# Threshold attention and a bilinear FFN on one core: turned weights moved per head, the last block's sums in column halves, VectorE and ScalarE ordered by a list scheduler

## The chip, the core and the metric

The kernel runs on one core of one Trainium2 chip. Its time is the device time of one execution in microseconds (us); lower is better. The engines are named as in the profile: PE is TensorE, PEld its weight load, DVE is VectorE, ACT is ScalarE, POOL is GpSimd, and SP is SyncE, which here does nothing but issue DMAs. Line numbers such as L411 are those of the kernel before.

## The reference

Two layers run one after the other. The first is attention with a threshold: only scores within `tau` of their row's maximum keep a weight. The second is a feed-forward layer that multiplies two projections.

```python
# q, k, v: (8 batches, 8 heads, 576 rows, 64); tau = 0.02
scores = (1 / np.sqrt(64)) * np.matmul(q, k.transpose(0, 1, 3, 2))
thresh = np.max(scores, axis=-1, keepdims=True) - tau
scores = np.where(scores >= thresh, scores, -1000000000.0)
attn = np.exp(scores - np.max(scores, axis=-1, keepdims=True))
attn = attn / (np.sum(attn, axis=-1, keepdims=True) + 1e-09)
out = np.matmul(attn, v)
x = out.transpose(0, 2, 1, 3).reshape(4608, 512)
# w_a, w_b: (512, 1536); w_out: (1536, 512)
return ((x @ w_a) * (x @ w_b)) @ w_out
```

## The kernel before

**Attention.** Heads are taken in pairs, so 32 pairs (8 batches of 4). A unit is a pair and a block of 128 query rows; the rows that are left over, 64 of each head, are put together from two pairs into a unit of their own ("tail", `u == NT`). There are 144 units. The main loop at the end of the kernel runs over slots `g`, one unit in each. A unit goes through these steps:

- `scores` (L404): PE multiplies q by k for both heads into two PSUM tiles `sc`. DVE takes the row maximum (`mx`, L411) and the threshold (`thr`, L412).
- `weigh`: ACT makes a bias (L431) and the exponential (L432); DVE sets to zero what lies under the threshold and sums the rows (L435). That is the last reading of `sc`.
- `reciprocal` and `normalise`: DVE (L446, L448), then ACT scales the weights `tw` by the reciprocal (L454).
- One slot later, `turn_blocks`: DVE transposes the weights within 32x32 blocks (L498), and DMAs write them to a tile `swap` in DRAM. The first eight units are turned on PE instead (`turn_pe`).
- Two slots later, `turn_back`: DMAs read `swap` into `wT`, where the turned weights have the keys on the partitions.
- Three slots later, `weighted` (L542): PE multiplies v by `wT` into a tile `pv`, and `settle` copies it to `xT`, one half by ACT (L549) and the other by DVE (L550).

**Feed-forward layer.** When the heads of 256 rows of a batch are there, they make a block of the layer (`ffn`). There are 18 of them. PE's work on them is laid between the steps of the units in portions (`advance`). Most blocks use a scheme with seven products in place of eight for a part of the projections (`sevens_of`, L720, the rest in L824) and for the output product (L885); sums and differences of operands stand in for the eighth, most of them made by POOL (L682, L853), and on DVE once the loop over the slots is over (`state["over"]`). Output rows leave through `rows_out`, which lists them, and `store`, which sends what is listed.

**The weights at the start.** They arrive in 36 pieces as 64-bit floats and are converted while the first units run: ACT (L298, L299), POOL (L305), DVE (L311, L319), POOL (L324).

**PSUM.** One pool of four buffers, called `banks`, serves all of PE's tiles (`tp`, `sc`, `pv`, `pab`, `po`).

**What sets the order.** `keep_order` ties every instruction to the one before it on its engine, in the order in which the program text emits them; so each engine works through its list in order. From slot 37 on, DMAs are not issued where they are posted: `post` puts them in a list, and `pump` issues from it as PE's columns pass, each tied to the matmul that was emitted last. `flush` issues what a step needs. All these DMAs go out on SP's queue; after the last slot SP and ACT take turns.

Of the kernel before, what the change touches and what calls it, by code (L numbers as in the profile page):

```python
# [37 lines left out]
BY_HEAD = 16  # L38


def keep_order(tc):

    last = {}
    for ins in tc.nc.cur_bb.bb.instructions:
        before = last.get(ins.engine)
        if before is not None:
            tc.add_manual_dep(
                ins, before,
                mybir.DependencyInfo(mybir.DependencyClass.NoSync, mybir.DependencyReason.DATA),
                reason="order")  # L50
        last[ins.engine] = ins.name
# [3 lines left out]
def kernel(  # L55
# [61 lines left out]

    def pool(name, bufs, **kw):
        return ctx.enter_context(tc.tile_pool(name=name, bufs=bufs, **kw))
# [32 lines left out]
    def pump(count=1, paced=True):  # L152

        for _ in range(min(count, len(bulk))):
            behind = next(x.name for x in reversed(nc.cur_bb.bb.instructions) if x.engine == mybir.EngineType.PE)
            for n, move in enumerate(bulk.pop(0)[2]):
                moved = nc.sync.dma_start(*move)
                if n == 0 and paced:
                    tc.add_manual_dep(
                        moved.ins, behind,  # L160
                        mybir.DependencyInfo(mybir.DependencyClass.Sync, mybir.DependencyReason.DATA),
                        reason="pace")
# [38 lines left out]
    def load_v(i, again=False):  # L201
        b, hp = pairs[i]
        if not again:
            loaded[i]["v"] = loads.tile([P, NSLOT, D], FP32, tag="vm", bufs=HP, name="vm")
        for j in range(2):
            rows, half = v[b, 2 * hp + j], loaded[i]["v"][j * D:(j + 1) * D]
            if i >= HP or again:
                if i < HP:
                    rows = rows.rearrange("(c s p) d -> p c s d", c=2, p=Q)
                else:  # L210
                    rows = rows.rearrange("(p c s) d -> p c s d", c=2, p=Q)
                post(("v", i), *((half[c * Q:(c + 1) * Q], rows[:, c]) for c in range(2)))
            else:
                nc.sync.dma_start(half, rows.rearrange("(s p) d -> p s d", p=D))
# [39 lines left out]
    def load_weights(limit, engine=nc.sync, most=NPIECES):  # L254
# [4 lines left out]
        while most and (len(raws) - len(taken) < limit or extra) and state["loaded"] < state["due"]:  # L259
# [7 lines left out]
            for r, part in enumerate(src):  # L267
# [4 lines left out]
                if behind and r == 0:  # L272
                    tc.add_manual_dep(
                        moved.ins, behind,
                        mybir.DependencyInfo(mybir.DependencyClass.Sync, mybir.DependencyReason.DATA),
                        reason="pace")
# [216 lines left out]
    def turn_blocks(i, u):  # L493
# [5 lines left out]
        swap = scratch.tile([G, P, NSLOT * Q], FP32, tag="swap" if u < NT else "swapt", name="swap")  # L499
        swaps[i, u] = swap  # L500
        for g in range(G):
            if u < NT:
                moves = [(swap[g].rearrange("(r p) e -> p r e", p=Q),
                          t[g * Q:(g + 1) * Q].rearrange("p (r s) e -> p r (s e)", r=G))]
            else:
                moves = []
                for m in range(2):
                    j = g // 2 ^ m
                    moves.append((swap[2 * m + g % 2, j * D:(j + 1) * D].rearrange("(r p) e -> p r e", p=Q),
                                  t[g * Q:(g + 1) * Q, m * NB:(m + 1) * NB].rearrange("p (r s) e -> p r (s e)", r=2)))  # L510
            post(("tw", i, u), *moves)

    def turn_back(i, u):

        key = "wT", i, min(u // 2, 1) if i >= HP else u // 2
        if u < NT or i < HP:
            flush(("tw", i, u))
            swap = swaps.pop((i, u)).rearrange("g p e -> p g e")
            turned[i, u] = turned_tile()
            for y in range(0, G, 2):  # L520
                post(key, (turned[i, u][:, y:y + 2].rearrange("p g s e -> p g (s e)"), swap[:, y:y + 2]))
# [277 lines left out]
    def ffn(xT, what):  # L799
# [51 lines left out]
        if state["sums"]:  # L851
# [4 lines left out]
            t1, t2, t4 = (sums_of[:, :, m] for m in range(3))  # L856

# [15 lines left out]
            for both in ((4, 1) if state["all"] else (1, 4), (2, 5), (7, 6), (3,)):  # L873
                po = banks(len(both) * CH, "po").rearrange("p r (m w) -> p r m w", w=CH)
                left = whole = len(both) * NF // 2 * CH
                for m in both:
                    y = sorted(both, reverse=7 in both).index(m)
                    k, u, other = seven[m]
                    for f in range(NF // 2):
                        ht = hs[f // 2 * 2 + k][:, f % 2]  # L880
                        for r in range(2):
                            rows = slice(r * D, (r + 1) * D)
                            for c in range(2):
                                t0 = u * P + c * D
                                nc.tensor.matmul(po[c * D:(c + 1) * D, r, y], ht[rows, t0:t0 + D],  # L885
                                                 other[rows, f], start=(f == 0), stop=(f == NF // 2 - 1))
                        left -= CH
# [4 lines left out]
                        if m == 2 and f == NF // 2 - 1:  # L892
                            h_sums((1, 0), (1, 0), (0, 0), ALU.subtract)
                            state["layer"] = False
                            exchange_blocks()
                        if left:
                            yield CH, left, whole
# [5 lines left out]
                elif 2 in both:  # L903
                    k25 = t
                    pool(k25[:, 0], k25[:, 0], k14[:, 0], op=ALU.add)
                elif 7 in both:
# [7 lines left out]
                else:  # L914
                    if state["over"]:
                        for r, t in enumerate((k76, k25)):
                            nc.vector.tensor_tensor(k25[:, 1], t[:, 1], po[:, r, 0], op=ALU.add)
# [4 lines left out]
                    written(0, k25)  # L922
# [23 lines left out]
    def rows_out(kind, b, h, u, t):  # L946

        if kind != "tail":
            r0 = b * S + h * HALF + u * P
            pending.append((out[r0:r0 + P, :], t))  # L950
        else:
            for e in range(2):
                r0 = (b + 2 * u + e) * S + MAIN
                pending.append((out[r0:r0 + TAIL, :], t[e * TAIL:(e + 1) * TAIL]))
# [102 lines left out]
    n = 0  # L1057
# [135 lines left out]
    keep_order(tc)  # L1193
# [32 lines left out]
```

## Time and profile before

| | |
|---|---|
| Median of 3 runs | 1419.77 us (1418.38 to 1431.88) |
| Span of the profiled execution | 1417.0 us |
| Distance of the median from that span | 2.8 us |
| PE busy | 1370.2 us (97%), 33836 instructions |
| PE weight load busy | 1229.6 us (87%) |
| DVE busy | 1013.7 us (72%), 2200 instructions |
| ACT busy | 679.9 us (48%) |
| POOL busy | 495.7 us (35%) |
| DMA moved | 223.20 MB in 327000 packets, 158 GB/s on average |
| Time of the packets on SP's queue, share of 16 DMA engines' span | 59.2% |
| Mean granted PE clock | 0.994 |

The profiled execution has no time of its own beside its span; the runs' times are 1.4 us and more above the span. Busy time is the time in which at least one instruction of the engine was under way. PE's instructions are two for each matmul of 32-bit numbers. An engine that is idle loses nothing unless the end of the kernel waits for it, so one looks for the engine on which the chain of waits runs, and then for the places where that engine stands still.

### The profile page before, as it was taken

What the parts mean: (1) busy time and instruction counts of PE and PEld (TensorE: products, weight loads), DVE (VectorE), ACT (ScalarE), POOL (GpSimd) and SP (SyncE); (2) the same over time, 40 slices, a digit from 0 to 9 for tenths busy, and PEclk for the clock granted to TensorE, in tenths of its full rate; (3) what the DMA queues carried; (4) which work ended last, traced back from release to release, by engine and by line L of the source; (5) the groups of instructions that cost most, each with busy time, mean ns of one, the idle gap of its engine ahead of it and who ended that gap; (6) DMA issues with size and microseconds to landing.
All of it is one profiled execution on the core that took longest, in us unless ns stands there. A gap on an engine that the chain in (4) does not pass through costs nothing.

```text
span 1417.0 us, 76257 instructions
## 1 busy us (share of the span) xinstructions
PE 1370.2 (97%) x33836; PEld 1229.6 (87%) x33836; DVE 1013.7 (72%) x2200; ACT 679.9 (48%) x1245; POOL 495.7 (35%) x678
## 2 busy tenths in 40 slices
PE   6788999999999999999999999999999999999998
PEld 5677579989878887979998999999888899799997
DVE  6898986778777877776767777677777776744424
ACT  5786554545445454545444545454545455431110
POOL 2674541606060606042333324150606060608100
PEclk9999999999999999999999999999999999999999
DMA  9967776667756775666555675567655775550000
GB/s 212 235 193 219 182 214 163 178 153 183 198 135 173 198 188 155 178 156 184 142 134 149 168 193 158 144 160 199 168 144 152 191 201 154 135 152 18 4 19 18
DMA packets 327000, 223.20 MB, mean 158 GB/s; under 512 B 171536, under 2 KB 310800, under 8 KB 326672
## 3 DMA queue, kind: packets, MB, share of 16 engines
q1 hardware_dynamic: 323712, 216.95, 59.2%
q8 instruction: 266, 4.36, 1.3%
q10 hardware_dynamic: 2960, 1.38, 0.4%
q14 instruction: 62, 0.51, 0.1%
HBM read 128.58 MB, written 89.65 MB: 154 GB/s over the span
## 4 chain that ended last, share of the span: by engine, by line
PE 86%; DVE 7%; DMA 3%; issue 2%; SPq 1%; ACT 0%; POOL 0%; DVEq 0%; POOLq 0%; ACTq 0%
PE pab L720 29%; PE po L885 20%; PE pab L824 16%; PE pv L542 10%; PE sc L404 10%; DVE mx L411 2%; DVE tw L498 2%; SPq L144 1%; DMA wT<-swap 1%; DVE tw L435 1%; PE tp L479 1%; DMA raw<-in_moe_w_a_dram 1%; DMA raw<-in_moe_w_b_dram 1%; DVE thr L412 0%; DVE u L790 0%
## 5 line engine op out<-in xcount | busy, mean ns | idle before, releaser
L411 DVE TENSOR_REDUCE mx<-sc 128x1 f32<-128x576 f32 x288 | 204.7, 752 | 125.8 <-PE sc L404 125.4
L454 ACT ACTIVATE tw<-tw,rcp 128x576 f32<-128x576 f32 x272 | 196.5, 770 | 202.3 <-DVE rcp L448 202.3
L682 POOL TENSOR_TENSOR h<-h,u 128x512 f32<-128x512 f32 x28 | 35.2, 1276 | 601.0 <-DVE h L794 426.1
L432 ACT ACTIVATE tw<-sc,bias,scalars 128x576 f32<-128x576 f32 x288 | 239.8, 833 | 10.9 <-PE pab L720 0.4
L435 DVE SCALAR_TENSOR_TENSOR tw<-sc,thr,tw 128x576 f32<-128x576 f32 x288 | 221.5, 799 | 10.4 <-ACT tw L432 9.9
L885 PE MATMUL po<-wo_sb,h 64*64 64x256 f32 x3264 | 205.8, 376 | 1.2 <-DVE h L794 1.1
L498 DVE STREAM_TRANSPOSE tw<-tw 128x576 f32<-128x576 f32 x272 | 194.4, 752 | 0.8 <-ACT tw L454 0.8
L885 PEld LDWEIGHTS po<-wo_sb,h 64*64 64x64 f32 x3264 | 157.0, 133 | 25.7 <-DVE h L794 2.6
L542 PE MATMUL pv<-wT,vm 64*64 64x160 f32 (+3 forms) x5184 | 169.2, 275 | 7.6 <-issue 3.6
L542 PEld LDWEIGHTS pv<-wT,vm 64*64 64x64 f32 x5184 | 157.4, 136 | 19.1 <-issue 9.8
L404 PE MATMUL sc<-kT,qT 64*64 64x288 f32 x2016 | 168.0, 404 | 1.1 <-DVE xt L550 0.5
L853 POOL TENSOR_TENSOR h<-h 128x256 f32<-128x256 f32 x168 | 117.4, 732 | 107.4 <-PE po L885 97.2
L885 PE MATMUL po<-sums_u,h 64*64 64x256 f32 x2448 | 153.4, 376 | 0.7 <-DVE h L832 0.7
L720 PE MATMUL pab<-xU,wb_sb 64*64 64x128 f32 x4352 | 138.0, 269 | 0.4 <-issue 0.3
L720 PEld LDWEIGHTS pab<-xU,wb_sb 64*64 64x64 f32 x4352 | 132.2, 133 | 3.7 <-issue 1.1
L885 PEld LDWEIGHTS po<-sums_u,h 64*64 64x64 f32 x2448 | 117.6, 133 | 19.4 <-DVE h L832 1.3
L404 PEld LDWEIGHTS sc<-kT,qT 64*64 64x64 f32 x2016 | 101.8, 133 | 22.6 <-issue 5.0
L549 ACT COPY xT<-pv 128x128 f32<-128x128 f32 (+1 forms) x68 | 17.7, 260 | 201.8 <-PE pv L542 200.2
L431 ACT ACTIVATE bias<-mx,scalars 128x1 f32<-128x1 f32 x288 | 83.1, 288 | 64.0 <-DVE mx L411 63.7
L550 DVE COPY xT<-pv 64x128 f32<-64x128 f32 (+1 forms) x136 | 38.1, 280 | 91.0 <-PE pv L542 89.7
L720 PE MATMUL pab<-xS,wa_sb 64*64 64x128 f32 x2176 | 101.8, 269 | 0.1
L531 ACT COPY kept<-po 128x512 f32<-128x512 f32 x65 | 34.8, 536 | 123.0 <-PE po L885 113.9
(156 smaller groups left out, 2414.3 us busy)
## 6 DMA issues: line engine op xcount, KB each, us to landing
wT<-swap SPq DMA_DIRECT2D x244, 288.0 KB, 3.9
swap<-tw SPq DMA_DIRECT2D x480, 144.0 KB, 2.9
vm<-in_v_dram SPq DMA_DIRECT2D x128, 72.0 KB, 2.5
swap<-tw SPq DMA_DIRECT2D x128, 72.0 KB, 3.0
kT<-in_k_dram SPq DMA_DIRECT2D x112, 72.0 KB, 3.3
wT<-swap SPq DMA_DIRECT2D x56, 144.0 KB, 3.3
out_dram<-kept SPq DMA_DIRECT2D x28, 256.0 KB, 3.9
qT<-in_q_dram SPq DMA_DIRECT2D x112, 40.0 KB, 2.8
```

What stands on the lines that cost most here:

```text
L404: nc.tensor.matmul(sc[m][o * D:o * D + wide, c], qT[r, q0:q0 + wide], kT[r, c * SH:(c + 1) * SH], start=True, stop=True)
L411: nc.vector.tensor_reduce(mx[:, c], sc[j], axis=AX.XY, op=ALU.max)
L431: nc.scalar.activation(bias[:, j:j + 1], mx[:, j:j + 1], AF.Copy, scale=e_nscale)
L432: nc.scalar.activation(wb[j], sb[j], AF.Exp, bias=bias[:, j:j + 1], scale=e_scale)
L435: nc.vector.scalar_tensor_tensor(out=wv, in0=sb[j], scalar=thr[:, j:j + 1], in1=wv, op0=ALU.is_ge, op1=ALU.mult, accum_out=sums[:, j:j + 1])
L454: nc.scalar.activation(w, w, AF.Copy, scale=rcp[:, j:j + 1])
L498: nc.vector.transpose(w, w)
L542: nc.tensor.matmul(pv[c * D:(c + 1) * D, y], vm[rows, s], wT[y](rows, s), start=(s == 0), stop=(s == NSLOT - 1))
L720: nc.tensor.matmul(out[c * D:(c + 1) * D, r, f * P:(f + 1) * P], w[g][k][rows, w0:w0 + D], moving[k][rows], start=(fresh and k == 0 and f ...
L824: nc.tensor.matmul(pab[c:c + columns(), r], w[rows, f // n, k, fs + c:fs + c + columns()], moving, start=(k == 0), stop=(k == H - 1))
L853: (nc.vector if state["over"] else nc.gpsimd).tensor_tensor(*a, **kw)
L885: nc.tensor.matmul(po[c * D:(c + 1) * D, r, y], ht[rows, t0:t0 + D], other[rows, f], start=(f == 0), stop=(f == NF // 2 - 1))
```

## The change

The change has three parts.

**Order.** `keep_order` is replaced by `order`. It goes through the instructions that the program text emitted, works out which depends on which (from the tiles and the parts of them that they read and write), and gives each an estimated cost. Then it lets the engines run by these costs: at each step it takes, over all engines, the instruction that can start first, where an engine may choose among its next `LOOK` instructions in the order of the text. For DVE and ACT that is 8, for PE, POOL and SP it is 1, so these three keep the order of the text. A tile can be opened only in the order of the text among the tiles of its kind, and when a buffer is free. The order that comes out is tied down as before. (`Book` only notes which tile comes from which pool.)

**Turned weights.** `turn_blocks` writes a head's weights in one DMA from all 128 partitions, 576 numbers in a run, in place of DMAs from 32 partitions each with runs of 288. The layout of `swap` follows, and in `turn_back` a read fills 64 partitions and four groups in place of 128 partitions and two groups. The rows of v follow the same order; from the fifth pair on they come in one DMA per pair.

**Last block's sums.** In the blocks whose output product starts after the last slot (`ending`), the last product (3) is made in two halves of 128 columns, each in a PSUM tile of its own. The sum of the other products for these rows is made before it, each half is added as it ends, and the finished halves of rows are stored separately.

The diff, cut to what matters:

```diff
+LOOK = {PE: 1, DVE: 8, Activation: 8, Pool: 1, SP: 1}
-def keep_order(tc):
-    ...
+def order(tc, slots, paced, look):
+    ...
+    while left:
+        best = None
+        for e, some in waiting.items():
+            ...
+            limit = mine[min(ahead[e] + look[e], len(mine)) - 1]
+            pick = None
+            for n in some:
+                if n > limit:
+                    break
+                at = room(n)
+                if at is None:
+                    continue
+                ...
+                at = max(at, safe[n], now[e])
+                if pick is None or at < pick[0]:
+                    pick = at, n, e
+                    if at <= now[e]:
+                        break
+            if pick and (best is None or pick[0] < best[0]):
+                best = pick
+        ...
@@ load_v
-            if i >= HP or again:
-                if i < HP:
-                    rows = rows.rearrange("(c s p) d -> p c s d", c=2, p=Q)
-                else:
-                    rows = rows.rearrange("(p c s) d -> p c s d", c=2, p=Q)
-                post(("v", i), *((half[c * Q:(c + 1) * Q], rows[:, c]) for c in range(2)))
+            if again:
+                rows = rows.rearrange("(c s p) d -> p c s d", c=2, p=Q)
+                post(("v", i), *((half[c:D:2], rows[:, c]) for c in range(2)))
+            elif i >= HP:
+                if j == 0:
+                    both = v[b, 2 * hp:2 * hp + 2].rearrange("j (q s) d -> (j q) (s d)", s=NSLOT)
+                    post(("v", i), (loaded[i]["v"].rearrange("p s d -> p (s d)"), both))
@@ turn_blocks
-        swap = scratch.tile([G, P, NSLOT * Q], FP32, tag="swap" if u < NT else "swapt", name="swap")
+        if u < NT:
+            swap = scratch.tile([2, P, S], FP32, tag="swap", name="swap")
+            for j in range(2):
+                post(("tw", i, u), (swap[j], t[:, j * NB:(j + 1) * NB].rearrange("p n e -> p (n e)")))
+        else:
+            ...
-        for g in range(G):
-            if u < NT:
-                moves = [(swap[g].rearrange("(r p) e -> p r e", p=Q),
-                          t[g * Q:(g + 1) * Q].rearrange("p (r s) e -> p r (s e)", r=G))]
-            else:
-                ...
-            post(("tw", i, u), *moves)
@@ turn_back
-            for y in range(0, G, 2):
-                post(key, (turned[i, u][:, y:y + 2].rearrange("p g s e -> p g (s e)"), swap[:, y:y + 2]))
+            for y in range(2):
+                if u < NT:
+                    rows, groups = slice(y * D, (y + 1) * D), slice(0, G)
+                    src = swap[y].rearrange("(g p) (c x) -> (p c) g x", g=G, c=2)
+                else:
+                    ...
+                post(key, (turned[i, u][rows, groups].rearrange("p g s e -> p g (s e)"), src))
@@ ffn, output product
+            ending = state["over"]
+                last = ending and 3 in both
+                for m, part in ((m, part) for m in both for part in range(1 + last)):
+                    cut = slice(part * CH // 2, (part + 1) * CH // 2) if last else slice(0, CH)
+                    if part:
+                        po = banks(CH, "po").rearrange("p r (m w) -> p r m w", w=CH)
...
+                        if last and f == NF // 2 - 1:
+                            for r in range(2):
+                                nc.vector.tensor_tensor(final[:, cut], final[:, cut], po[:, r, 0, cut],
+                                                        op=ALU.add)
+                                if not part:
+                                    second(r)
...
+                    if ending:
+                        pool(k25[:, 1], k25[:, 1], k14[:, 0], op=ALU.add)
+                        pool(k14[:, 0], k14[:, 0], k14[:, 1], op=ALU.add)
+                        rows_out(kind, b, h, 0, k25[:, 0], slice(0, CH))
+                elif 7 in both and ending:
+                    k76, final = t, keep("kept")[:, 1]
+                    pool(final, k76[:, 1], k25[:, 1], op=ALU.add)
+                    def second(r):
+                        if not r:
+                            pool(k76[:, 1], k76[:, 0], k76[:, 1], op=ALU.add)
+                            nc.gpsimd.tensor_tensor(k14[:, 0], k76[:, 1], k14[:, 0], op=ALU.add)
+                        else:
+                            pool(k14[:, 1], k76[:, 1], k25[:, 1], op=ALU.add)
+                            written(1, k14)
...
-                    if state["over"]:
-                        for r, t in enumerate((k76, k25)):
-                            nc.vector.tensor_tensor(k25[:, 1], t[:, 1], po[:, r, 0], op=ALU.add)
+                    if ending:
+                        rows_out(kind, b, h, 0, final, slice(CH, DM))
...
-    keep_order(tc)
+    order(tc, slots, after_of, LOOK)
```

## The prediction

> **What bounds the kernel now.** I read the page first (busy shares, slices, chain), then the stretches of the span, then who waits for whom, then VectorE's timeline in an early and a late place, then the end.
>
> ```profile
> PE 1370.2 (97%) x33836; PEld 1229.6 (87%) x33836; DVE 1013.7 (72%) x2200; ACT 679.9 (48%) x1245; POOL 495.7 (35%) x678
> ...
> PE 86%; DVE 7%; DMA 3%; issue 2%; SPq 1%; ACT 0%; POOL 0%; DVEq 0%; POOLq 0%; ACTq 0%
> ```
>
> PE is busy for 97% of the span and holds 86% of the chain; no part of the change removes work from it. So the most that can be won is PE's idle time, 1417.0 - 1370.2 = 46.8 us, and the question is where it lies.
>
> ```profile
> 0.00:20.00 20.00, 10.95 (x56) 8.11 (x58) 8.36 (x22) 8.21 (x15) 1.93 (x8) 1.00 1.07 204
> 20.00:120.00 100.00, 81.90 (x1564) 71.92 (x1561) 92.16 (x203) 79.49 (x163) 64.56 (x73) 0.97 0.93 221
> 120.00:200.00 80.00, 75.55 (x1252) 52.76 (x1253) 69.54 (x152) 46.81 (x91) 44.15 (x35) 0.96 0.75 194
> 200.00:1300.00 1100.00, 1091.26 (x27627) 989.07 (x27623) 803.15 (x1754) 532.02 (x958) 367.99 (x540) 1.00 0.62 163
> 1300.00:1417.00 117.00, 110.54 (x3359) 107.69 (x3350) 40.47 (x73) 13.37 (x22) 17.07 (x23) 0.98 0.05 17
> ```
>
> The columns are the stretch, its length, the busy times of PE, weight load, DVE, ACT and POOL with their instructions, PE's granted clock, the DMA share and GB/s. PE is idle for 9.1 us in the first 20, 18.1 in the next 100, 4.5 from 120 to 200, 8.7 in the 1100 us after that, and 6.5 at the end. From 20 to 120 us DVE is the fullest engine: 92.16 of 100.
>
> ```profile
> DVE mx L411 <- PE sc L404: 125.4, 108, 4.4
> ...
> DVE xT L550 <- PE pv L542: 89.7, 56, 3.7
> ...
> PE pv L542 <- DMA wT<-swap: 2.9, 1, 2.9
> ```
>
> DVE runs in program order and stands for 125.4 us in front of the row maximum L411, whose scores are not there yet, and 89.7 us in front of L550, whatever is ready behind them. PE itself waits once for a turned weight from DMA, 2.9 us.
>
> **The change part by part.**
>
> **1. Order of DVE and ACT.** Between the two programs PE, POOL and SP keep their order. Of 1924 DVE instructions 1325 stand elsewhere, by at most 7 places: the transposes L498 three places earlier on average, the conversions L311 and L319 two and one earlier, L411 and L412 two later, the copies L550 two later. Durations and counts stay. What this does is seen at 25 us:
>
> ```profile
> 25.34 1.42 DVE L411 TENSOR_REDUCE mx<-sc 128x1 f32<-128x576 f32 x2 [0.45 <-PE sc L404]
> ...
> 28.22 0.68 DVE L311 SCALAR_TENSOR_TENSOR low<-raw,low 128x512 uint32<-128x512 uint32 x1
> 28.82 0.42 DVE L319 TENSOR_SCALAR wa_sb<-wa_sb 128x512 uint32<-128x512 uint32 x1
> 29.15 0.81 DVE L435 SCALAR_TENSOR_TENSOR tw<-sc,thr,tw 128x576 f32<-128x576 f32 x1
> ```
>
> The pair L311, L319 (1.02 us) now stands six places earlier, ahead of this L411; its inputs were there from 23.7 and 23.9 us. It starts in the 0.45 us gap, L411 starts about 0.6 later, and L435, whose exponential ended at 27.9, need not wait for the pair. Such pairs move ahead of L411 near 18, 25, 33, 57 and 67 us. DVE idles 2.4 us at 15.6 and 7.8 us from 20 to 120 (100 - 92.16): 10.2 is the cap there, since its work stays. I take the pair's 1.0 where the gap is longer than it (16, and two of those from 60 to 80) and the gap where it is shorter (0.45, 0.39, 0.47), less 0.1 per place for a late handover: 3.0 + 1.3 - 0.5 = **3.8**, bounds 0 to 10. Zero comes if the weights' transfers bind: the DMA share is 0.93 here and over 1 before 20 us.
>
> From 120 to 200 us PE idles 4.5; 2.9 of it is the wait of part 2. Of the other 1.6 I take **1.0**, bounds -1 to 1.6.
>
> After 200 us a typical slot reads:
>
> ```profile
> 406.82 0.17 DVE L448 RECIPROCAL rcp<-sums 128x2 f32<-128x2 f32 x1
> 409.08 1.42 DVE L411 TENSOR_REDUCE mx<-sc 128x1 f32<-128x576 f32 x2 [2.10 <-PE sc L404]
> 410.54 0.74 DVE L412 TENSOR_SCALAR thr<-mx,scalars 128x2 f32<-128x2 f32 x1
> 411.19 1.43 DVE L498 STREAM_TRANSPOSE tw<-tw 128x576 f32<-128x576 f32 x2
> 412.55 0.64 DVE L532 TENSOR_TENSOR kept<-kept,po 128x512 f32<-128x512 f32 x1
> ```
>
> The two L498 have their input at 407.8 and 408.5 (ACT's L454), and now run in the 2.10 us hole. L411 starts 0.2 later, and L435, which gives the two PSUM banks of the scores back, can start with its exponential at 412.1 instead of 413.54. Where L454 ends later than the scores, L411 is pushed back instead: by the times of this trace the second L498 is ready over 0.5 us after the scores for 128 of 239 L411, and two L498 cost 1.50 us. PE notices only where it is waiting for a bank: of 457 PSUM tiles opened from 200 to 1280 us, 75 got a bank freed under 1 us before, 30 of them by L435. PE's idle time there is 8.7 us, the cap. I take a quarter, **2.2**, because early and late releases nearly balance; bounds -20 to 8.7 (the loss is priced under the rivals).
>
> ACT's moves go with these: its L549 copies stand three places later, but ACT idled 200 us before them, and the bank needs DVE's L550 as well.
>
> One rule speaks of what such moves cost. L412 took 0.228 us in the median and 2.05 at most, L319 0.41 to 1.51, with POOL at work beside them. The Trainium skill, "SBUF — State Buffer", section "Who interferes with whom", says a DVE operation in a two-port mode and a GpSimd one exclude each other for whole instructions and that issue order decides who blocks; by it a new order draws new collisions. It would add or take some tenths of a microsecond at a place, with no sign, and the sum goes without it.
>
> **2. Turned weights.** A unit's write to `swap` was four DMAs of 144 KB from 32 partitions each, and becomes two of 288 KB over all 128; the tail's eight of 72 KB become four. Reading back stays two DMAs of 288 KB in the same runs, but each now fills 64 partitions with four groups where it filled 128 with two. V comes in one DMA in place of four for pairs 4 and up. SP issues 1102 in place of 1488. The bytes stay, so the DMA engines' 59.2% should stay about. An issue on SP has a median of 0.39 us; 386 fewer are 151 us of a queue that mostly waits for PE on purpose (the pacing), so nothing but latency comes of it. PE feels it where it waits: near 123 us. There SP issued four `swap` in 2.25 us and then the read at 120.62 (landing 6.0 us later). Two issues fewer are 1.1 us: **1.1**, bounds -1 to 2.9 (the whole wait). One landing of 288 KB takes 3.9 us, one of 144 KB 2.9, and the writes ran side by side, so a unit's write may land up to 1 us later and eat the gain; elsewhere the cover is that a read is issued a slot ahead of its use, and if that were gone each of some 120 units could lose that 1 us.
>
> A rule speaks against the read-back. The Trainium skill, "SBUF — State Buffer", section "Door 1: The DMA port swizzle", holds that 64 adjacent partitions reach only half of the ports (196 GB/s against 328 at 1 MiB). By it a 288 KB read would take an estimated 1.5 us instead of 0.9 in the data, two of them 1.2 more, and this part would give nothing; the sum would be 1.1 smaller. No row here has both shapes at one size, so I leave it aside.
>
> **3. Last block.** Three blocks take the new path: their last product is cut in two column halves, 96 matmuls of 128 columns for 48 of 256. At 1325 in 36.35 us and 336 in 18.13 that is 2.63 for 2.59 us each: +0.1 in all.
>
> ```profile
> 1410.42 0.96 POOL L910 TENSOR_TENSOR kept<-kept 128x256 f32<-128x256 f32 x1 [53.74 <-DVE kept L853]
> 1411.46 0.72 POOL L911 TENSOR_TENSOR kept<-kept 128x256 f32<-128x256 f32 x1
> ...
> 1412.21 0.88 DVE L917 TENSOR_TENSOR kept<-kept,po 128x256 f32<-128x256 f32 x2 [1.42 <-POOL kept L911]
> ```
>
> PE ends at 1410.66. Then L917 waits for POOL, ends at 1413.09, and 3.9 us of issue and landing follow. Afterwards one POOL addition is left, and the last rows are ready as half tiles. DVE's new row: join to 1409.43, one 0.43, half 0.26 (from 0.42 for 256), 0.43, 0.26, 0.43, two halves 0.52 = 1411.8; POOL's 0.96 ends at 1411.6. The first pair of stores is issued at 1411.85, the last (0.51 each) at 1412.35 in place of 1413.1, with half the bytes. Gain 0.75 + 0.3 = **1.0** net, bounds 0.5 to 1.8.
>
> **Sum.** 3.8 + 1.0 + 2.2 + 1.1 + 1.0 = 9.1 us off the profiled 1417.0: 1407.9. The runs' median, 1419.8, lies 2.8 above that span; carried over with that distance: **1410.7 us**.
>
> **The rivals.**
> A. The order frees PE more than I count. For it: most moved conversions had their input 3 to 6 us before, and DVE's holes are long. Against: the DMA share over 1 early. With 8 of the 10.2, 1.6, 5, 2.9 and 1.0 it is 18.5: 1401.3.
> B. Hidden anyway: DMA binds the start, PE's 8.7 us stay. Only parts 2 and 3 are left, 2.1: 1417.7. For it: PE at 99.2% after 200 us. Against: the five gaps.
> C. Slower: L411 is held behind L498 in the 128 late cases, the scores' banks come back later, and PE stands in front of them. Price: up to 1.5 us for each; half swallowed by L435 waiting for ACT anyway, and 30 to 40% of the units near a bank limit give 0.2 to 0.3 us for each of 123 units, 25 to 37 us; with the other gains of 6.9, some 1438 to 1450. It cancels my forecast from 0.07 us a unit (9.1 / 123), and is over 1% from 0.17. Against: in the late cases the reciprocal L448 moves earlier too, which brings L454 forward.
> D. The new order does not act, since buffers still pin it: this is B's number.
>
> **How the numbers follow.** Forecast 0.40 (1405 to 1415, of which 0.02 under 1405.6); A 0.35; B and D 0.12; C 0.13, of which 0.02 stay within 1%. A measurement of this kernel tells about 1%, 14.2 us, from no change. Faster 0.35 + 0.02 = 0.37; slower 0.11; within 0.38 + 0.12 + 0.02 = 0.52. The low end takes all upper bounds, 10 + 1.6 + 8.7 + 2.9 + 1.8 = 25: 1394.8, cut to 1396; the high end reaches 6 us into C's slope, 1425, leaving its prices out.
>
> **What would show it.** Right: PE idle from 20 to 120 us near 14; DVE's wait for the scores far below 125 us; the wait for `wT` under 2; the last store issued near 0.8 us sooner after PE's end. Wrong: PE idle over 12 us after 200 us with waits named L435 or L550 (C), conversions on ACT waiting for `raw` in the first 70 us (B), or reads of `wT` landing over 5 us with PE behind them.

## The result, and the profile after

The changed kernel takes 1432.71 us in the median of 7 runs (1431.04 to 1434.48), the kernel before 1422.21 us (1414.55 to 1431.88, 7 runs beside them). The ratio is 1.0086, with a 95% interval of 1.0064 to 1.0109. It is slower by 0.9%, where 0.6% faster was forecast. The profiled span is 1430.1 us against 1417.0.

The page of the kernel after (busy time, then the chain):

```profile
PE 1372.0 (96%) x33980; PEld 1239.5 (87%) x33980; DVE 1056.3 (74%) x2212; ACT 681.6 (48%) x1245; POOL 494.8 (35%) x675
...
PE 84%; DVE 10%; DMA 2%; issue 2%; ACT 1%; SPq 1%; DVEq 0%
```

PE's busy time grew by 1.8 us only, so 11.3 of the 13.1 us are idle time. DVE is busy for 42.6 us more with almost the same instructions, and its share of the chain rose from 7 to 10%. The stretches of the span (columns as above) tell where PE stood:

```profile
20.00:120.00 100.00, 81.53 (x1548) 72.56 (x1548) 94.41 (x197) 80.18 (x163) 65.21 (x73) 0.95 0.93 225
120.00:200.00 80.00, 73.71 (x1258) 50.16 (x1249) 74.43 (x153) 45.36 (x88) 44.33 (x34) 1.00 0.77 197
200.00:1300.00 1100.00, 1081.19 (x27385) 991.89 (x27389) 821.50 (x1738) 532.83 (x957) 356.84 (x523) 1.00 0.60 162
```

PE idles 18.5 us from 20 to 120 (18.1 before), 6.3 to 200 (4.5), and 18.8 in the 1100 us after that (8.7), which is most of the loss. Who PE waited for, kernel after (total, times, longest):

```profile
PE pab L963 <- issue: 7.9, 14, 1.2
...
PE pab L1067 <- DVE tw L673: 4.5, 4, 2.1
...
PE sc L642 <- ACT h L1073: 2.4, 1, 2.4
```

L963 was L720 before, L1067 L824, L642 L404 and L673 L435. The top row is the new one. Kernel before, the rows of this kind:

```profile
PE pv L542 <- issue: 3.6, 4, 1.8
...
PE pab L720 <- issue: 1.2, 3, 0.6
```

"issue" means that PE stopped with nothing to wait for that the profile shows. The last wait for a turned weight fell from 2.9 us to 0.7. DVE's waits, kernel after:

```profile
DVE xT L793 <- PE pv L785: 69.0, 46, 3.7
DVE tw L736 <- ACT tw L692: 64.4, 89, 1.6
DVE mx L649 <- PE sc L642: 49.1, 53, 3.5
DVE tw L673 <- ACT tw L670: 36.0, 98, 1.6
```

The wait in front of the row maximum (L649, before L411) did fall, from 125.4 to 49.1 us, as the new order means to. In its place DVE now waits for ACT: 64.4 us in front of the transposes (L736, before L498) and 36.0 in front of L673 (9.9 before). The DMA issues, kernel after (count, size, us to landing):

```profile
wT<-swap SPq DMA_DIRECT2D x244, 288.0 KB, 4.7
swap<-tw SPq DMA_DIRECT2D x240, 288.0 KB, 4.2
```

And before:

```profile
wT<-swap SPq DMA_DIRECT2D x244, 288.0 KB, 3.9
swap<-tw SPq DMA_DIRECT2D x480, 144.0 KB, 2.9
```

### The profile page after: what moved, and what is told of

Read it like the earlier page. It is cut to its first block, busy times and chain, and to the rows that moved or that the text cites. A ratio compares the mean times of both kernels' runs of the same rounds, so it can differ in the third digit from the quotient of the medians.

```text
span 1430.1 us, 75672 instructions
## 1 busy us (share of the span) xinstructions
PE 1372.0 (96%) x33980; PEld 1239.5 (87%) x33980; DVE 1056.3 (74%) x2212; ACT 681.6 (48%) x1245; POOL 494.8 (35%) x675
## 3 DMA queue, kind: packets, MB, share of 16 engines
q8 instruction: 267, 4.37, 1.3%
## 4 chain that ended last, share of the span: by engine, by line
PE 84%; DVE 10%; DMA 2%; issue 2%; ACT 1%; SPq 1%; DVEq 0%
PE pab L963 29%; PE po L1133 21%; PE pab L1067 16%; PE sc L642 9%; PE pv L785 9%; DVE mx L649 2%; DVE tw L673 2%; DVE tw L736 1%; DVE low L549 1%; DVE thr L650 1%; DMA raw<-in_moe_w_a_dram 1%; DMA raw<-in_moe_w_b_dram 1%; DMA sums_u<-in_moe_w_a_dram 1%; DVE xT L793 0%; DVE wa_sb L557 0%
## 5 line engine op out<-in xcount | busy, mean ns | idle before, releaser
L692 ACT ACTIVATE tw<-tw,rcp 128x576 f32<-128x576 f32 x272 | 197.7, 769 | 198.5 <-DVE rcp L686 197.8
L673 DVE SCALAR_TENSOR_TENSOR tw<-sc,thr,tw 128x576 f32<-128x576 f32 x288 | 229.4, 809 | 41.1 <-ACT tw L670 36.0
L736 DVE STREAM_TRANSPOSE tw<-tw 128x576 f32<-128x576 f32 x272 | 201.0, 764 | 66.3 <-ACT tw L692 64.4
L649 DVE TENSOR_REDUCE mx<-sc 128x1 f32<-128x576 f32 x288 | 202.0, 741 | 49.3 <-PE sc L642 49.1
L1133 PE MATMUL po<-wo_sb,h 64*64 64x256 f32 (+1 forms) x3408 | 212.9, 367 | 1.7 <-DVE thr L650 1.7
L1133 PEld LDWEIGHTS po<-wo_sb,h 64*64 64x64 f32 x3408 | 162.1, 133 | 24.7 <-POOL xS L808 2.1
L642 PE MATMUL sc<-kT,qT 64*64 64x288 f32 x2016 | 175.7, 404 | 6.1 <-ACT h L1073 2.4
L1133 PE MATMUL po<-sums_u,h 64*64 64x256 f32 x2448 | 158.9, 376 | 0.0
L1096 POOL TENSOR_TENSOR h<-h 128x256 f32<-128x256 f32 x168 | 117.3, 732 | 116.2 <-PE po L1133 115.1
L963 PE MATMUL pab<-xU,wb_sb 64*64 64x128 f32 x4352 | 140.5, 269 | 1.0 <-issue 1.0
L963 PEld LDWEIGHTS pab<-xU,wb_sb 64*64 64x64 f32 x4352 | 134.7, 133 | 3.6 <-issue 2.1
L642 PEld LDWEIGHTS sc<-kT,qT 64*64 64x64 f32 x2016 | 106.0, 133 | 26.9 <-issue 5.0
L963 PE MATMUL pab<-xS,wa_sb 64*64 64x128 f32 x2176 | 110.9, 269 | 0.1
L963 PE MATMUL pab<-xT,wa_sb 64*64 64x128 f32 x1856 | 93.8, 269 | 1.2 <-issue 1.2
L963 PEld LDWEIGHTS pab<-xS,wa_sb 64*64 64x64 f32 x2176 | 91.2, 133 | 1.3 <-issue 0.8
L1067 PE MATMUL pab<-xT,wb_sb 64*64 64x256 f32 (+2 forms) x1184 | 87.4, 374 | 4.6 <-DVE h L1075 3.0
```

Of the source, the lines that this page charges most:

```text
L642: nc.tensor.matmul(sc[m][o * D:o * D + wide, c], qT[r, q0:q0 + wide], kT[r, c * SH:(c + 1) * SH], start=True, stop=True)
L649: nc.vector.tensor_reduce(mx[:, c], sc[j], axis=AX.XY, op=ALU.max)
L673: nc.vector.scalar_tensor_tensor(out=wv, in0=sb[j], scalar=thr[:, j:j + 1], in1=wv, op0=ALU.is_ge, op1=ALU.mult, accum_out=sums[:, j:j + 1])
L692: nc.scalar.activation(w, w, AF.Copy, scale=rcp[:, j:j + 1])
L736: nc.vector.transpose(w, w)
L963: nc.tensor.matmul(out[c * D:(c + 1) * D, r, f * P:(f + 1) * P], w[g][k][rows, w0:w0 + D], moving[k][rows], start=(fresh and k == 0 and f ...
```

## The stops called issue

One of them, in the timeline of PE, kernel after (start, duration, then the idle time before):

```profile
506.67 0.55 PE L963 MATMUL pab<-xU,more_u 64*64 64x128 f32 x12 [1.22 <-issue]
```

PE is in the middle of a stream of equal matmuls here, it waits for no semaphore, and it stands for 1.22 us. What it lacks, as the following shows, is its instructions. Queue q8 is called "instruction" by the page:

```profile
q8 instruction: 267, 4.37, 1.3%
```

These are 4.37 MB in 267 packets of 16 KB. PE and its weight load have 2 x 33980 instructions, and 4.37 MB over them is 64 bytes each. So this queue brings PE's program while it runs. In the streams of L963, 64 matmuls took 2.13 us, so a packet (some 127 matmuls with their weight loads) is used up in an estimated 4.2 us; over the whole span one lasts 5.4 us (1430 / 267).

I counted the places after 200 us where one matmul starts over 0.3 us later than the one before it allows (these sums are a little larger than PE's idle time) and that have no recorded wait. In the kernel after, 19 of 20 begin again 1.2 to 1.6 us after a packet of q8 ended; before 6 of 6, in e2 28 of 28, in e15 20 of 20. Such a packet ends every 5.4 us, so chance would put about one in thirteen into a window of 0.4 us. I call these stops for instructions: before 3.6 us, after 15.3 us. All other stops after 200 us went from 13.3 to 14.7. (These sums move by about 1 us with how the start that the matmul before allows is worked out.)

## The experiments

All ratios are against the kernel before on the same chip, with 95% intervals. The diffs show only the lines that matter, mostly without `rearrange`.

### Which part: e1, e2, e3, e4

e1 has the new order alone (old transfers and last block), e2 the new transfers alone, e3 the new last block alone (look-ahead 1 everywhere). e4 is the whole change with `LOOK` of ScalarE at 1.

```diff
 # e4
-LOOK = {PE: 1, DVE: 8, Activation: 8, Pool: 1, SP: 1}
+LOOK = {PE: 1, DVE: 8, Activation: 1, Pool: 1, SP: 1}
```

> The new order of VectorE and ScalarE alone, with the transfers and the last block of the kernel before. Two theories. Fetch theory: the loss comes from TensorE standing without instructions, 5 such stops of 3.3 us in all after 200 us before and 18 of 14.8 us after, each ending 1.2 to 1.6 us after a fetch of instructions landed; the larger transfers cause them. Then this kernel has 3 to 8 such stops and is within 5 us of the kernel before (ratio 0.997 to 1.0035). Order theory: the order itself costs, through copies out of PSUM that stand behind the exponential or the scaling on ScalarE (stops of 2.7 us at 201, 1.5 at 170, 1.0 at 131); then it is 5 to 12 us slower (ratio 1.0035 to 1.0085) with the stops before instructions as few as before.

> The turned weights written and read per head and the v loads in one transfer, with the order and the last block of the kernel before. Fetch theory: the stops before instructions after 200 us rise to 12 to 20 of 10 to 16 us, and the kernel is 6 to 12 us slower (ratio 1.004 to 1.0085). Order theory: these stops do not depend on the transfers but on when they are issued, so they stay at about 5 and the kernel is 0 to 2 us faster.

> The last block's sums in column halves alone. Both theories: 0.5 to 1.5 us less between the last matmul and the end, TensorE's idle time elsewhere as before; the ratio is 0.999 to 1.0.

> The changed kernel with the list scheduler looking ahead on VectorE alone; ScalarE keeps the order of the text. Fetch theory: the stops before instructions stay (12 to 20 after 200 us), ScalarE's late copies go (the 2.7 us at 201 and the 1.5 at 170), so it is 3 to 5 us faster than the changed kernel and 5 to 10 us slower than before. Order theory with ScalarE as the culprit: it is level with the kernel before or faster.

e1 came out at 0.9996 [0.9972, 1.0021], e2 at 1.0067 [1.0041, 1.0093], e3 at 0.9999 [0.9975, 1.0023], e4 at 1.0102 [1.0059, 1.0144]. So the loss comes with the transfers, the part that was priced at 1.1 us of gain; the three parts alone add up to 0.62%. The order gains nothing, and its stops for instructions are 9.4 us on the old transfers (3.6 before), which is more of them than the 3 to 8 of the fetch theory. Taking ScalarE's look-ahead away doesn't help: e4 was expected 3 to 5 us faster than the changed kernel, and isn't. PE's waits in e2:

```profile
PE pab L726 <- issue: 11.4, 19, 1.5
```

Its stops for instructions are 24.7 us, with the old order, and more than the 10 to 16 expected. In e3 the time from PE's end to the kernel's end is 5.3 us, against 6.3 before.

### Which part of the transfers: e5, e6, e7, e8

```diff
 # e5, from e2: write in runs of 1152 B, read unchanged
-swap = scratch.tile([2, P, S], ...)
+swap = scratch.tile([2, P, 2, SH + 16], ...)
 # e6, from e2: each write split by 32 partitions (8 of 72 KB)
-post(("tw", i, u), (swap[j], t[:, ...]))
+for z in range(4):
+    rows = slice(z * Q, (z + 1) * Q)
+    post(("tw", i, u), (swap[j][rows], t[rows, ...]))
 # e7, from before: four reads of 144 KB for two of 288
-for y in range(0, G, 2):
-    post(key, (turned[i, u][:, y:y + 2], swap[:, y:y + 2]))
+for y in range(G):
+    post(key, (turned[i, u][:, y:y + 1], swap[:, y:y + 1]))
 # e8, from before: reads into 64 partitions, four groups
+for y in range(2):
+    rows = slice(y * D, (y + 1) * D)
+    post(key, (turned[i, u][rows, 0:G], swap[rows]))
```

> As e2 (new transfers, old order and last block), but swap has a gap of 16 numbers between the halves of a row, so that one write of 288 KB goes out in 256 runs of 1152 B in place of 128 runs of 2304 B. If the length of a run makes TensorE's instruction fetches late, the stops go back to the 3 to 10 us of the kernel before and the time to within 4 us of it (ratio under 1.003). If it is the size of one transfer (18 KB for each of 16 engines), they stay at 12 to 25 us and the ratio at 1.004 to 1.009.

> As e2, but each head's write goes out as four transfers of 72 KB from 32 partitions each, runs of 2304 B kept: eight issues a unit. Size theory: the write holds an engine for 4.6 KB at a time, less than the 9.2 KB of the kernel before, so stops of 2 to 10 us and a time level with the kernel before or up to 5 us faster (ratio 0.996 to 1.002). Run-length theory: the stops stay at 12 to 25 us, ratio 1.004 to 1.009. That the v loads or the reads into 64 partitions are the cause: also 1.004 to 1.009.

> The kernel before with only the read-back cut finer: four reads of 144 KB, one group each, in place of two of 288 KB. Size theory: it goes the other way than the change, stops for instructions at 0 to 4 us after 200 us and 2 to 6 us faster than before (ratio 0.996 to 0.999). If only writes matter, it is level (0.999 to 1.001). If the issues on SyncE bind, it is slower by 1 to 5 us with longer waits for wT.

> The kernel before with one edit: the two reads of a unit's turned weights fill 64 partitions and four groups each, as in the change, in place of 128 partitions and two groups; writes, v loads, runs and sizes of the reads stay (288 KB, 1152 B). Read theory: reads into half of the partitions hold up TensorE's instruction fetches; stops of 12 to 25 us after 200 us, wT landing in 4.7 us as after the change, ratio 1.005 to 1.010. Write theory (the larger writes did it): stops of 3 to 10 us, landing 3.9 us, ratio 0.998 to 1.002.

e5: 1.0094 [1.0068, 1.0120]; the length of the runs isn't it. e6: 1.0443 [1.0414, 1.0472], and e7: 1.0150 [1.0117, 1.0184]; both issue more DMAs on SP, and PE stands for late weights: 11.6 us in e6, 6.4 in e7 (2.9 before). Both were expected level or faster by the size theory; the third theory, that SyncE's issues bind, had 1 to 5 us of loss for e7, where it is some 21. Waiting isn't all of it: PE is also busy longer, 1387.3 us in e6 and 1384.9 in e7 (1370.2 before), at a granted clock of 0.984 and 0.983 (0.994). So splitting the transfers brings a cost of its own and can't clear their size; but e7 has only 4.8 us of stops for instructions. e8 changes nothing but which partitions a read fills, with the same bytes, runs and number of DMAs, and gives 1.0115 [1.0079, 1.0152]. PE's waits in e8:

```profile
PE pab L721 <- issue: 11.7, 17, 1.5
...
PE pv L543 <- DMA wT<-swap: 5.3, 4, 3.3
```

That is no less than the loss of e2, without any other part of it. Its profiled span is 22.7 us longer than that of before: PE is idle for 14.8 us more and busy for 7.9 more, at a granted clock of 0.990.

### A better shape: e9, e10

e9 keeps the long runs of the change (2304 B), but writes 32 partitions of both heads in each of four DMAs, and reads into 128 partitions and two groups as before. Order and last block are the old ones. e10 is the changed kernel with these transfers.

```diff
 # e9 (from e2), e10 (from the kernel after)
-swap = scratch.tile([2, P, S], ...)
-for j in range(2):
-    post(("tw", i, u), (swap[j], t[:, j * NB:(j + 1) * NB].rearrange("p n e -> p (n e)")))
+swap = scratch.tile([G, P, NSLOT * Q], ...)
+rows = swap.rearrange("g (j p c) x -> g p j (c x)", j=2, c=2)
+for g in range(G):
+    post(("tw", i, u), (rows[g], t[g * Q:(g + 1) * Q].rearrange("p (j n) e -> p j (n e)", j=2)))
...
-    rows, groups = slice(y * D, (y + 1) * D), slice(0, G)
+    rows, groups = slice(0, P), slice(2 * y, 2 * y + 2)
```

> Runs of 2304 B and the v loads in one transfer, as in the change, but a write takes both heads of 32 partitions (four of 144 KB a unit) and the reads fill 128 partitions and two groups, as before; old order and last block. Read theory and size theory: stops of 3 to 10 us, level with the kernel before, ratio 0.997 to 1.002. If the v load in one piece (288 KB) is the cause: stops of 12 us or more, ratio 1.004 to 1.009.

> The changed kernel (new order, new last block, one v load) with the transfers of e9 in place of those of the change. Read theory: the loss of the change goes, so 0 to 4 us faster than the kernel before (ratio 0.997 to 1.000) with stops for instructions of 3 to 10 us. Write theory: the same, since these writes are small again. If the order costs together with the transfers: ratio 1.004 or more.

e9: 0.9960 [0.9944, 0.9975], with `wT` landing after 3.5 us and 2.6 us of stops for instructions. e10: 1.0003 [0.9986, 1.0019] and 3.2 us of stops. What makes e9 faster than the kernel before, the longer runs or the v loads in one transfer, was not separated. From e10 to the changed kernel (1.0086) it is the shape of the transfers alone, 0.8%.

### The order again, on good transfers: e12, e13, e14

e12 is e9 with the new last block and look-ahead 1; e13 and e14 give VectorE or ScalarE alone the look-ahead of 8.

```diff
 # e12: DVE 1, Activation 1;  e13: DVE 8;  e14: Activation 8
-LOOK = {PE: 1, DVE: 8, Activation: 8, Pool: 1, SP: 1}
+LOOK = {PE: 1, DVE: 1, Activation: 1, Pool: 1, SP: 1}
```

> The transfers of e9 with the new last block and the order of the text on all engines. e10 differs from it in the order alone. Order costs: it is 4 to 7 us faster than e10 and 5 to 8 us faster than the kernel before (ratio 0.9945 to 0.9965). Order is neutral: it is within 2 us of e10 (ratio 0.999 to 1.0015). TensorE's end to the end of the kernel: 5.2 us.

> As e12, with the look-ahead of 8 on VectorE alone. If what the order costs is VectorE's doing (its busy time in sum rises by 25 us, from 1121 to 1146 to 1148, in operations that meet GpSimd), it lies at e10 (ratio 1.000 to 1.002), with the sum of VectorE's durations at 1143 to 1150. If it is ScalarE's late copies out of PSUM, it lies at e12 (ratio 0.995 to 0.997).

> As e12, with the look-ahead of 8 on ScalarE alone. VectorE as the cause: level with e12 (ratio 0.995 to 0.997), VectorE's sum at 1120. ScalarE as the cause: 3 to 6 us slower than e12 (ratio 0.999 to 1.001), with waits of TensorE for L792 and L1073.

e12: 0.9957 [0.9934, 0.9979], faster than the kernel before (1420.06 us against 1427.24 on that chip). e13: 1.0011 [0.9989, 1.0033]. e14: 0.9984 [0.9963, 1.0005]. So VectorE's new order costs 0.5% here, and ScalarE's gains nothing. A part of the cost shows early: PE is idle from 20 to 200 us for 21.9 us in e12 and 22.9 in e14, and for 26.8 in e13 and 25.5 in e10. Of all kernels with the two reads into 128 partitions, the six without VectorE's look-ahead lie at 20.5 to 22.9 us there, and the three with it (e1 is the third) at 24.7 to 26.8. The rest the profiles don't settle. From 200 to 1300 us PE is idle for 11.1 us in e12, 17.6 in e13, 12.7 in e14 and 13.0 in e10, and most of what e13 has more are stops for instructions, with the same transfers. PE's waits in e12, then in e13:

```profile
PE pab L960 <- issue: 2.3, 6, 1.0
```

```profile
PE pab L960 <- issue: 8.0, 16, 1.3
```

The profile of e13 is of its slowest run (1437.01 us, the median is 1428.94), so it may overstate this.

### Adjacent or every second partition: e11, e15, e16, e17

e11 is e8 with rows 0, 2, 4 ... and 1, 3, 5 ... in its two reads. e15 and e16 do the same two things to e9, and e17 is e9 itself, on one chip with them.

```diff
 # e15 (from e9; e8 is this on before)
-    post(key, (turned[i, u][:, groups], swap[groups]))
+    rows = slice(y * D, (y + 1) * D)
+    post(key, (turned[i, u][rows, 0:G], swap[:, rows]))
 # e16 (from e15; e11 is this on e8)
-    rows = slice(y * D, (y + 1) * D)
+    rows = slice(y, P, 2)
```

> As e8, but the 64 partitions of a read are every second one (0, 2, 4 ... and 1, 3, 5 ...) in place of the lower and the upper half. Number, size and runs of the reads are those of e8. Half theory: it is the crowding into one half of the partitions that slows a read and with it the fetches; then wT lands in 3.6 to 4.1 us, the stops after 200 us are 3 to 10 us, and the time is level with the kernel before (ratio 0.998 to 1.003). Group theory: four groups for a partition are what slows it; then all is as in e8, landing 4.6 to 4.9, stops 15 to 25 us, ratio 1.006 to 1.012.

> The kernel of e9 (runs of 2304 B, writes of 32 partitions from both heads, reads into 128 partitions and two groups: 0.9960) with one change: each read fills 64 adjacent partitions and four groups. If the shape of the read alone costs, as e8 said: landing of wT from 3.5 back to 4.5 us or more, 15 us or more of stops for instructions after 200 us, and a ratio of 1.006 to 1.012. If the loss in e8 came from its own chip or its run-to-run spread (stops for instructions were 2.6 to 13.5 us in runs with the same reads): a ratio near 0.997 and under 12 us of stops.

> As e15, but each read fills every second partition (0, 2, 4 ... and 1, 3, 5 ...). If the loss is that 64 adjacent partitions are behind half of the ways in, all of it goes: landing of wT 3.5 to 3.9 us, stops under 12 us, ratio 0.995 to 0.998. If 64 partitions of any kind cost (each read then holds half of the keys for both heads, and fewer partitions take more from each row), part of it stays: 1.000 to 1.006, as e11 suggested with 1.0061 against 1.0115 of e8.

> The kernel of e9 once more, beside e15 and e16 on the same chip, as the point that both are measured from: 0.994 to 0.998 and stops for instructions of 2 to 12 us after 200 us. If it comes out at 1.000 or above, the gain of e9 was spread between chips and nothing under half a per cent can be told.

| | reads of `wT` fill | landing, us | stops for instructions after 200 us | ratio |
|---|---|---|---|---|
| e17 | 128 partitions, 2 groups | 3.6 | 3.5 us | 0.9965 [0.9947, 0.9983] |
| e16 | every second, 4 groups | 3.9 | 5.0 us | 1.0007 [0.9987, 1.0028] |
| e15 | 64 adjacent, 4 groups | 4.7 | 15.9 us | 1.0091 [1.0056, 1.0126] |
| e11 (old layout) | every second, 4 groups | 4.0 | 12.7 us | 1.0061 [1.0038, 1.0085] |

PE's waits in e17, then in e15:

```profile
PE pab L723 <- issue: 2.3, 5, 1.1
```

```profile
PE pab L723 <- issue: 9.0, 14, 1.5
...
PE pv L545 <- DMA wT<-swap: 2.9, 2, 2.4
```

And the queues of e17, then of e15 (packets, MB, share of 16 DMA engines' time):

```profile
q1 hardware_dynamic: 286528, 216.94, 58.2%
```

```profile
q1 hardware_dynamic: 286528, 216.94, 61.7%
```

The same packets with the same bytes take 61.7% of the DMA engines' time in place of 58.2 (e16: 58.1). The packets of 1152 bytes, most of which are these reads, took, from 200 to 1280 us, 77 ns in the mean in e15 and 62 in e17 (e16: 63). So adjacent partitions make each packet slower, and every second partition mends that. This agrees with the Trainium skill, "SBUF — State Buffer", section "Door 1: The DMA port swizzle": 64 adjacent partitions reach half of the 16 ports, and by its table every second partition reaches all of them. Of the 1.3% between e15 and e17, 0.8 go with adjacency. The 0.4 that stay in e16 are not explained, and the profiles can't show them: that of e16 is of a run 5 us under its median (1416.38 us, 1421.74), that of e17 of one 4 us over its own (1418.26, 1414.51). On the old layout, too, every second partition brings back the landing (4.0 us) but only about half of the time: e11 lost 0.6% where e8 lost 1.15%, and was expected level if the crowding were all. So the crowding into half of the partitions is shown as a part of the loss, and not as all of it.

Over all runs, the stops for instructions are 15.3 to 24.7 us in the seven kernels that read into 64 adjacent partitions (after, e2, e4, e5, e6, e8, e15), and 2.6 to 13.5 us in the ten that read into 128. So they also vary with no change of shape: 3.5 and 2.6 us in the two profiles of one kernel (e17, e9), 13.5 in e13 with the same transfers, 9.4 and 9.6 in e1 and e3, whose transfers are those of before (3.6).

## Why the prediction was wrong

**Step 2 failed in size and sign.** The sum had 1.1 us of gain for the transfers; alone they cost 0.67%, some 9.5 us (e2). The wait that it named did shrink: near 123 us PE stands for 1.8 us in e2, for ACT, in place of the 2.9 for `wT`, so the 1.1 was there. What failed is the list of waits. "PE feels it where it waits: near 123 us" let the transfers reach PE through late weights alone. The rule of the Trainium skill on adjacent partitions ("SBUF — State Buffer", section "Door 1: The DMA port swizzle") was likewise taken only as a later landing of `wT`, priced at 1.1, and left aside. The landing of one read grew by 0.8 us (3.9 to 4.7), and in e2 PE waits for none. But PE also waits for something else that DMA brings, its own program, and that I had not put on the list. The kernel before could have told: its page has the row of q8, and two of its four "issue" stops in front of L542, 2.4 of the 3.6 us, end 1.5 and 1.6 us after a packet of q8. The cover that I named (a read is issued a slot ahead) hides late weights and not late instructions. No rival named this wait either; C, the one that forecast a slower kernel, goes by the scores' banks.

How slower reads hold the instructions back is shown in part only. A packet of q8 takes about as long in e15 (1.11 us in the mean) as in e17 (1.09), so the delay must lie ahead of it. In before, after, e2, e8 and e15 the DMA engines were busy with queue q1, the kernel's own transfers, for 0.82 to 0.92 of the 2 us ahead of those q8 packets that ended a stop, and for 0.62 to 0.73 of the 2 us ahead of the others. That fits a fetch that comes late where transfers crowd the engines; what holds it there has no record in the trace.

**Step 1, the order, failed too: no gain on the old transfers, a loss on those of e9.** 7.0 us of gain were forecast. e1 shows a change of -0.6 us (interval -4.0 to +3.0), and on the transfers of e9 VectorE's part alone loses 0.54%, 7.7 us (e13 against e12, one chip). The step that failed took a gap of DVE that is filled as time that PE gains, at unchanged durations. PE's idle time from 20 to 120 us, where 3.8 us were to be won, went from 18.1 to 19.0 in e1 and 18.5 after; the prediction's sign of being right was 14. (The 3.8 itself takes off 0.1 for five places, where six are listed.) The place that the prediction showed, DVE in the kernel after:

```profile
24.13 0.68 DVE L549 SCALAR_TENSOR_TENSOR low<-raw,low 128x512 uint32<-128x512 uint32 x1
24.74 1.51 DVE L557 TENSOR_SCALAR wa_sb<-wa_sb 128x512 uint32<-128x512 uint32 x1
26.16 1.41 DVE L649 TENSOR_REDUCE mx<-sc 128x1 f32<-128x576 f32 x2
...
28.36 0.82 DVE L673 SCALAR_TENSOR_TENSOR tw<-sc,thr,tw 128x576 f32<-128x576 f32 x1
...
29.77 0.81 DVE L673 SCALAR_TENSOR_TENSOR tw<-sc,thr,tw 128x576 f32<-128x576 f32 x1
```

The pair (L549 and L557, before L311 and L319) moved ahead of the row maximum as predicted, but L557 took 1.51 us in place of 0.42, beside POOL's L562, which ran from 24.30 to 25.96. The maximum starts at 26.16 in place of 25.34, 0.8 later and not 0.6. The first L673 is 0.8 sooner; the second, which frees the other bank, ends at 30.58 against 30.62. Nothing is won.

In the next stretch, from 120 to 200 us, where 1.0 us of gain was taken, PE's idle time went from 4.5 to 6.3 us. Late in it the new order loses outright. Kernel after, the timeline from 197 us on:

```profile
197.32 2.35 POOL L920 TENSOR_TENSOR more_u<-wa_sb,more_u 128x1024 f32<-128x1024 f32 x1
...
197.58 2.12 DVE L684 TENSOR_SCALAR sums<-sums 128x2 f32<-128x2 f32 x1
...
199.73 0.17 DVE L686 RECIPROCAL rcp<-sums 128x2 f32<-128x2 f32 x1
199.93 0.77 ACT L692 ACTIVATE tw<-tw,rcp 128x576 f32<-128x576 f32 x1 [4.51 <-DVE rcp L686]
...
200.61 0.56 ACT L1073 COPY h<-pab 128x512 f32<-128x512 f32 x1
...
201.23 0.47 PE L642 MATMUL sc<-kT,qT 64*64 64x288 f32 x4 [2.37 <-ACT h L1073]
```

L684 (L446 before) works on two numbers per partition. It began 0.26 us after POOL's addition, and ended 0.03 us after it: 2.12 us. Behind it stood the reciprocal, behind that ACT's L692, behind that the copy L1073, which gives PE a bank, and PE lost 2.37 us. L684 takes 0.17 us in the mean where no POOL work overlaps it, before and after. Where POOL does, it is 0.35 before (51 of 136) and 0.49 after (60 of 136), with 7 over 1 us in place of 1. The groups of this line in e12, then in e13:

```profile
L684 DVE TENSOR_SCALAR sums<-sums 128x2 f32<-128x2 f32 x136 | 31.2, 230 | 3.3
```

```profile
L684 DVE TENSOR_SCALAR sums<-sums 128x2 f32<-128x2 f32 x136 | 39.6, 292 | 3.4
```

So it comes with VectorE's look-ahead. All DVE durations together are 1146.0 us after and 1121.3 before (1141.2 in e13 and 1124.8 in e12). In each of these four traces, every DVE instruction that took over 0.1 us more than the median of its shape had POOL at work beside it; what these took beyond that median is 37.0 us before and 53.7 after, 39.5 in e12 and 50.0 in e13. The prediction cited the rule for this (the Trainium skill, "SBUF — State Buffer", section "Who interferes with whom"); L684's end, 0.03 us after POOL's, agrees with it. But "some tenths of a microsecond at a place, with no sign" was my own figure and wrong: it is up to 2 us, and in sum it was longer. "Durations and counts stay" failed. That these collisions are the 0.5% is argued and not shown: e1 has them too (durations of 1139.0 us, 49.8 beyond the medians), and by its time lost nothing.

After 200 us, 2.2 of gain were taken. PE's waits for L673 (L435 before) and the other stops there barely moved (13.3 to 14.7 us), so rival C's mechanism, banks coming back late behind the transposes, is not what made it slower either, though PE's idle time after 200 us passed the 12 us that stood as its sign. DVE's holes were filled and reopened as waits for ACT, and PE gained nothing from it.

**Step 3 was right.** From PE's end to the kernel's end it was 6.3 us and is 5.2, 1.2 less where 1.0 was forecast (bounds 0.5 to 1.8). The last store is issued 1.67 us after PE's end, where it was 2.45: 0.8 sooner, as forecast. The time of e3 is too blunt to show 1 us. POOL, DVE and ACT's queue at the end, kernel after:

```profile
1424.97 0.72 POOL L1171 TENSOR_TENSOR kept<-kept 128x256 f32<-128x256 f32 x1 [54.80 <-DVE kept L1096]
1425.00 0.97 DVE L1096 TENSOR_TENSOR kept<-kept 128x256 f32<-128x256 f32 x1
1425.89 0.59 DVE L1146 TENSOR_TENSOR kept<-kept,po 128x128 f32<-128x128 f32 x2
1426.06 1.40 ACTq L379 DMA_DIRECT2D out_dram<-kept  x2
```

The half sums are there; L1096, beside POOL's last addition, took 0.97 us and not the 0.42 of the one before it.

**The sum.** Read one after the other, the 0.86% split so: longer runs and the new last block on good reads -0.43% (e12), the order +0.46% (e10), the shape of the transfers with their reads +0.83% (after). Each of these differences is known to some 0.3%, and the three kernels were measured on different chips, each against before.

## What to carry to other kernels

Where PE runs at 97% of the span with small matmuls, as here, its program is one of the transfers: look at the "issue" stops and the instruction queue before calling a DMA change hidden. Fill all the partitions in a read rather than half of them side by side, even if nobody waits for the read; every second partition mended only a part here. When an order moves small DVE instructions, ask what POOL is doing at the new place; a hole that is filled on an engine off the path is no gain.

## What was not expected of the hardware

- PE's instructions come by DMA while it runs, 16 KB at a time in packets of 1.1 us, and PE starts again 1.2 to 1.6 us after one has ended. Slower reads of other data, which use no more bytes, raised these stops from 3.5 to 15.9 us (e17, e15).
- Splitting transfers into more and smaller ones on one queue cost more than their shape: eight writes of 72 KB per unit in place of two of 288 KB made 1.0443 of 1.0067 (e6, e2).
- A VectorE instruction of 0.17 us took 2.12 us beside one POOL addition.
